# Weight conversion spread over a step, an early rescale on ScalarE, and single eighths in two of nine steps

## The chip, the cores and the metric

The kernel runs on one core of a Trainium2 chip. Time is that of one execution on the device, in microseconds; a kernel's time is the median of its runs. A profiled execution is traced by the hardware profiler, and its span runs from the first to the last instruction of the program.

## The reference

Three layers follow one another on float32 data: attention that keeps the 32 highest scores of each row, a gated feed-forward layer, and a layer of eight experts in which each token goes to one. Cut to what matters:

```python
# attention: 4 batches, 8 heads, 576 rows, 64 wide
scores = q @ k.T / sqrt(64)
kth = np.partition(scores, -32, axis=-1)[..., -32:-31]
scores = np.where(scores >= kth, scores, -1e9)
attn = exp(scores - scores.max(-1))
attn = attn / (attn.sum(-1) + 1e-9)
x = attn @ v                          # as 2304 tokens of 512
# feed-forward: w_in 512x2048, w_out 2048x512, given as float64
h = x @ w_in
x = (h * clip(h + 3, 0, 6) / 6) @ w_out
# experts: each token to the one of 8 with the highest logit, 512 -> 1024 -> 512
out[mask] = gate[mask] * (relu(x[mask] @ w1[e]) @ w2[e])
```

## The kernel before

**Steps and units.** Attention is cut into 72 units: 64 of two heads by 128 query rows (`t`), and 8 for the remaining rows of four heads (`r`). A loop of 76 steps runs them as a pipeline of five stages written out by hand: step i makes the scores of unit i (stage 0), selects the 32 highest of unit i-1 on VectorE, masks unit i-2, exponentiates and rescales unit i-3, and transposes unit i-4 and multiplies it with V. The order in which `step` calls the pieces is the order of each engine's instructions; every engine takes its own in order and waits at semaphores for the others. Four score buffers `s` go round.

Per step, VectorE runs four rounds of MAX and MATCH_REPLACE (`select`, L354 and L357), the reciprocal of the row sums (L388) and `pairs` (L335 to L339), which halves the rows that the next `select` looks at. `pairs` reads the score copy that ScalarE makes (`take`, L326) and the scores in PSUM, and TensorE can write the next scores only when it is through. ScalarE also does `relu` (L371), `expo` (L381) and the copies of the transposes (`keep`, L410); GpSimd does `mask` (L375) and the rescale (`scale`, L394).

**Feed-forward work in the same steps.** A group of 128 tokens is finished with each fourth `t` unit of a batch and row block (two more groups with the last `r` unit), and puts eight eighths into the queue `moe`; an eighth is 256 of the 2048 hidden columns. A step takes up to two, `a` and `b`: `s1` is 16 products with w_in into PSUM (L463), `gate`, `swish`, `large` and `small` (L468 to L479) make the gated value in two parts, and `s2` is six products with w_out (L488). Of `a`, all of it stands in one step; the `s2` of `b` stands in the next step, as `last`. A step that finds the queue empty starts none. What is left after the loop is taken by a loop behind it, ahead of the experts.

**Weight conversion.** w_in and w_out arrive as 64-bit words, in 64 pieces of 128x256, each by a DMA into one of five raw buffers (`load_w`). `convert_w` takes two pieces: VectorE shifts and masks the high words (L194, a TENSOR_SCALAR) and joins the sign (L196); then, for three of four pieces, ScalarE scales the low word (L199) and GpSimd adds it (L200), for the fourth VectorE joins it (L202). A w_in piece is finished with that. A w_out piece goes into a buffer `wf` of a ring of four that it shares with the gate's tile `u`; ScalarE then rounds it into `wh` (L204) and GpSimd puts the rest into `wl` (L205), in the same call. The calls stand at the end of a step: two in steps 0 to 3, three in steps 4 to 7, four from step 8, so the 64 pieces are through with step 10.

Of the kernel before, what the change touches and what calls it, by code (L numbers as in the profile page):

```python
# [25 lines left out]
CH = 256  # L26
# [8 lines left out]
BIG = 2.0 ** 100  # L35
NUNIT = 72
NS = 4
HS = S // 2
QS = S // 4
SCALE = 1.0 / 8.0  # L40
# [23 lines left out]
def layers(ctx: ExitStack, tc: tile.TileContext, qt, kt, v, w_in, w_out, embt, tau, w1, w2, out, y_dram, g_dram, x_dram, tbl, flag):  # L64
# [93 lines left out]
    for q in range(8):  # L158
        for k in range(4):
            c = slice(256 * q, 256 * q + 256)  # L160
            wpieces.append((w_in[128 * k:128 * k + 128, c], win[:, k, c], None))
        for k in (2 * q, 2 * q + 1):
            for c in (slice(0, 256), slice(256, 512)):
                wpieces.append((w_out[128 * k:128 * k + 128, c], wh[:, k, c], wl[:, k, c]))
    wraw = deque()
    cnt = [0]

    def load_w():
# [11 lines left out]
    def convert_w():  # L180


        plain, words = [], []
        for raw, dst, rest, single in [wraw.popleft() for _ in range(min(2, len(wraw)))]:
            full = dst if rest is None else mp.tile([128, 256], F32, tag="ug", name="wf", bufs=4)
            if single:
                nc.vector.tensor_copy(full, raw)
            else:
                cnt[0] += 1
                words.append((raw, full.bitcast(I32), cnt[0] % 4 != 3))  # L190
            if rest is not None:
                plain.append((full, dst, rest))
        for raw, t, _ in words:
            nc.vector.tensor_scalar(t, raw[:, :, 1], 3, 0x3FFFFFF8, op0=ALU.logical_shift_left, op1=ALU.bitwise_and)  # L194
        for raw, t, _ in words:
            nc.vector.scalar_tensor_tensor(t, raw[:, :, 1], -0x40000000, t, op0=ALU.bitwise_and, op1=ALU.bitwise_or)  # L196
        for raw, t, rounded in words:
            if rounded:
                nc.scalar.activation(raw[:, :, 0], raw[:, :, 0].bitcast(U32), AF.Copy, scale=2.0 ** -29)  # L199
                nc.gpsimd.tensor_tensor(t, t, raw[:, :, 0], op=ALU.add)  # L200
            else:
                nc.vector.scalar_tensor_tensor(t, raw[:, :, 0], 29, t, op0=ALU.logical_shift_right, op1=ALU.bitwise_or)  # L202
        for full, hi, lo in plain:
            nc.scalar.copy(hi, full)  # L204
            nc.gpsimd.tensor_tensor(lo, full, hi.bitcast(F32), op=ALU.subtract)  # L205
        load_w()

# [91 lines left out]
    def lows():  # L301
        while low:
            o, x, h = low.popleft()
            nc.gpsimd.tensor_tensor(o, x, h, op=ALU.subtract)
        while low2:
            o, x, h = low2.popleft()
            nc.vector.tensor_tensor(o, x, h, op=ALU.subtract)  # L307
# [82 lines left out]
    def scale(i):  # L390
        rv = sums.pop(i)
        for n in range(2):
            x = tile_of(i, n)
            nc.gpsimd.tensor_scalar(x, x, rv[:, n:n + 1], 1.0, op0=ALU.mult, op1=ALU.mult)  # L394

    tb_ = {}

# [56 lines left out]
    def push_group(X, g):  # L454
# [9 lines left out]
            state[q, "h"] = ph.rearrange("p a n -> p (a n)")  # L464

        def gate(q):
            state[q, "u"] = u = mp.tile([128, CH], F32, tag="ug", name="u", bufs=4)
            nc.scalar.activation(u, state[q, "h"], AF.Relu, bias=half, scale=1.0 / 6.0)  # L468

        def swish(q):  # L470
# [223 lines left out]
    def step(i, last):  # L694
        def at_(j, f, *a):
            if 0 <= i - j < NU:
                f(i - j, *a)

        a = moe.popleft() if moe else None
        b = moe.popleft() if moe else None  # L700
        part(last, 4)
        part(last, 5)
        at_(2, relu, 0)
        at_(2, mask, 0)
        at_(3, expo, 0)
        lows()
        load_k(i + 2)
        at_(1, select, 0)
        at_(1, select, 1)
        part(a, 1)  # L710
        part(a, 2)
        part(a, 3)
        for c in range(2):
            at_(4, turned, c)
            at_(4, keep, c)
        at_(0, scores, 0)
        at_(4, turned, 2)
        at_(4, keep, 2)
        at_(0, take, 0)
        at_(1, select, 2)  # L720
        at_(3, expo, 1)
        at_(3, guard)
        part(last, 6)
        part(a, 4)
        part(a, 5)
        at_(0, scores, 1)
        at_(0, take, 1)
        at_(1, select, 3)
        at_(3, inverse)
        at_(3, scale)  # L730
        at_(2, relu, 1)
        at_(2, mask, 1)
        at_(1, bounds)
        part(b, 1)
        at_(0, pairs)
        part(b, 2)
        part(b, 3)
        load_q(i + 3)
        if i + 1 < NU and units[i + 1][0] == "r":
            prep(i + 1)  # L740
            lows()
        if i + 2 < NU and units[i + 2][0] != "r":
            prep(i + 2)
        at_(4, values)
        part(a, 6)
        at_(4, finish)
        need_v(i)
        if side:
            side.popleft()()
        if i == 1:  # L750
            setup()
        if i == 5:
            embed()
        for _ in range(2 if i < 4 else 3 if i < 8 else 4):
            convert_w()
        return b or a

    if True:
        for t in zq:
# [232 lines left out]
```

## Time and profile before

| | |
|---|---|
| median of 3 runs | 1216.61 us (1215.84 to 1221.48) |
| the profiled execution | 1215.63 us, its span 1213.9 us |
| TensorE (PE) products busy | 1045.8 us, 86% of the span |
| VectorE (DVE) busy | 835.2 us, 69% |
| ScalarE (ACT) busy | 735.2 us, 61% |
| GpSimd (POOL) busy | 664.9 us, 55% |

Busy time is a mean over stages: the first 200 us convert weights, the next 600 run attention and feed-forward together, and the last 400 the rest of the feed-forward layer and the experts. Products are pipelined and their ends modelled, so a busy TensorE is not one at its peak. An idle gap is put down to the engine or DMA whose signal came last before it ended.

### The profile page before, as it was taken

To read this page: it belongs to the slowest core of one execution; us is meant where nothing else is said; L and a number is where in the kernel's file an instruction comes from. 1 tells how busy PE (TensorE), PEld (TensorE's weight loads), DVE (VectorE), ACT (ScalarE), POOL (GpSimd) and SP (SyncE) were. 2 spreads that over 40 slices of the span, in tenths; PEclk is the share of its full clock that TensorE was granted. 3 is DMA by queue.
4 is the path that set the end of the run, shared out by engine and by line. 5 is a ranking of instruction groups with operands and counts; after the bars stand their busy time and mean duration, and the time that the engine had idled before them with its cause. 6 is when DMAs were issued, how large, how long until landed. Compare 5 with 4: busy or idle time off the path is not lost.

```text
span 1213.9 us, 22599 instructions
## 1 busy us (share of the span) xinstructions
PE 1045.8 (86%) x7800; PEld 927.7 (76%) x7800; DVE 835.2 (69%) x2718; ACT 735.2 (61%) x1628; POOL 664.9 (55%) x950
## 2 busy tenths in 40 slices
PE   2244659998999989999998999999998899999993
PEld 1133548887989878899887999988987788877882
DVE  6989777899878799887989878861234343444540
ACT  4455547787777788777777777774344343443540
POOL 5767666687666687766778567663330343221200
PEclk9976778999999999999999999999998999999997
DMA  7433230131000132000131000100040564333530
GB/s 221 136 94 122 89 100 25 47 82 55 11 27 25 32 91 62 10 28 25 42 86 56 10 27 21 30 10 10 10 165 10 173 213 177 133 132 123 186 140 21
DMA packets 71782, 92.75 MB, mean 76 GB/s; under 512 B 18319, under 2 KB 44066, under 8 KB 71647
## 3 DMA queue, kind: packets, MB, share of 16 engines
q1 hardware_dynamic: 67007, 81.00, 21.1%
q0 software_dynamic: 4640, 10.10, 2.5%
q8 instruction: 66, 1.08, 0.4%
q14 instruction: 69, 0.57, 0.2%
HBM read 80.37 MB, written 11.32 MB: 76 GB/s over the span
## 4 chain that ended last, share of the span: by engine, by line
PE 46%; issue 10%; DMA 8%; DVE 7%; ACT 5%; POOL 2%; SPq 1%; POOLq 0%; ACTq 0%; DVEq 0%
PE bank_h L463 15%; PE y L488 13%; PE bank_a L423 5%; DMA out_dram<-ob,idt 5%; PE ps_sc L323 4%; PE bank_t L405 3%; PE ph L821 3%; DVE A L354 2%; PE po L834 2%; DMA a<-in_moe_w_dram 1%; PE bank_t L517 1%; DVE left L357 1%; ACT s L381 1%; DMA xg<-y_dram,idt 1%; DVE kst L307 1%
## 5 line engine op out<-in xcount | busy, mean ns | idle before, releaser
L463 PE MATMUL bank_h<-x,win 128*128 128x128 f32 x2304 | 291.4, 279 | 5.0 <-ACT x L443 3.6
L463 PEld LDWEIGHTS bank_h<-x,win 128*128 128x128 f32 x2304 | 280.7, 195 | 12.0 <-ACT x L443 4.3
L375 POOL TENSOR_TENSOR s<-s,z 128x576 f32<-128x576 f32 x144 | 185.5, 1288 | 3.7 <-ACT z L371 3.5
L405 PE MATMUL bank_t<-ident,s 128*128 128x128 f32 x648 | 102.2, 286 | 79.4 <-ACT pt L410 71.4
L354 DVE MAX8 A<-left 128x8 f32<-128x288 f32 (+1 forms) x288 | 160.2, 598 | 0.0
L479 POOL TENSOR_TENSOR gl<-u,gh 128x256 fp32r<-128x256 f32 x144 | 106.5, 740 | 84.2 <-ACT gh L476 78.3
L405 PEld LDWEIGHTS bank_t<-ident,s 128*128 128x128 f32 x648 | 76.2, 147 | 89.1 <-ACT pt L410 79.1
L468 ACT ACTIVATE u<-bank_h,half 128x256 f32<-128x256 f32 x144 | 68.0, 472 | 110.0 <-PE bank_h L463 106.2
L488 PE MATMUL y<-wh,gh 128*128 128x512 f32 x288 | 128.9, 447 | 0.0
L323 PE MATMUL ps_sc<-kst,qh 128*128 128x288 f32 x256 | 85.0, 345 | 43.5 <-ACT s L326 24.1
L394 POOL TENSOR_SCALAR s<-s,sums 128x576 f32<-128x576 f32 x144 | 106.4, 749 | 24.0 <-DVE sums L388 23.9
L488 PE MATMUL y<-wh,gl 128*128 128x512 f32 x288 | 116.2, 403 | 0.0
L472 DVE SCALAR_TENSOR_TENSOR u<-u,bank_h 128x256 f32<-128x256 f32 x144 | 59.9, 416 | 81.4 <-ACT u L468 80.5
L488 PE MATMUL y<-wl,gh 128*128 128x512 f32 x288 | 115.2, 400 | 0.0
L653 DVE TENSOR_TENSOR l<-a,h 128x1024 fp32r<-128x1024 f32 x64 | 76.7, 1222 | 56.0 <-ACT h L652 55.8
L371 ACT ACTIVATE z<-s,zb 128x576 bf16<-128x576 f32 x144 | 112.5, 781 | 0.0
L410 ACT COPY pt<-bank_t 128x384 f32<-128x384 f32 x216 | 96.2, 480 | 26.7 <-PE bank_t L405 26.7
L381 ACT ACTIVATE s<-s,nb 128x576 f32<-128x576 f32 x144 | 111.8, 776 | 0.0
L326 ACT COPY s<-ps_sc 128x576 f32<-128x576 f32 x144 | 92.9, 645 | 17.0 <-PE ps_sc L323 17.0
L423 PE MATMUL bank_a<-pt,vt 128*64 128x128 f32 (+1 forms) x1600 | 99.5, 274 | 0.0
L385 POOL TENSOR_SCALAR sums<-sums 128x2 f32<-128x2 f32 x72 | 15.9, 220 | 148.9 <-ACT s L381 148.0
L323 PEld LDWEIGHTS ps_sc<-kst,qh 128*128 128x128 f32 x256 | 52.5, 205 | 57.1 <-ACT s L326 19.7
(222 smaller groups left out, 2513.4 us busy)
## 6 DMA issues: line engine op xcount, KB each, us to landing
a<-in_moe_w_dram SPq DMA_DIRECT2D x64, 512.0 KB, 7.9
kraw<-in_k_dram SPq DMA_DIRECT2D x64, 144.0 KB, 2.5
qraw<-in_q_dram SPq DMA_DIRECT2D x64, 128.0 KB, 2.2
w<-in_moe_w_in_dram SPq DMA_DIRECT2D x32, 256.0 KB, 3.1
w<-in_moe_w_out_dram SPq DMA_DIRECT2D x32, 256.0 KB, 2.8
vt<-in_v_dram SPq DMA_DIRECT2D x16, 320.0 KB, 3.1
y_dram<-ysb SPq DMA_DIRECT2D x18, 256.0 KB, 2.0
qraw<-in_q_dram SPq DMA_DIRECT2D x16, 64.0 KB, 2.0
```

Of the source, the lines that this page charges most:

```text
L323: nc.tensor.matmul(ps[:, n, :HS], t, kk[:, HS * g:HS * g + HS], start=(o == 0), stop=(o == len(parts) - 1))
L354: nc.vector.max(A[:, n, 8 * r:8 * r + 8], src[:, n, :w])
L371: nc.scalar.activation(zb_[n], tile_of(i, n), AF.Relu, bias=sel[i][2][:, n:n + 1], scale=-BIG)
L375: nc.gpsimd.tensor_tensor(s, s, zb_[n], op=ALU.subtract)
L381: nc.scalar.activation(s, s, AF.Exp, bias=sel[i][1][:, n:n + 1], scale=SCALE, accum_out=sums[i][:, n:n + 1])
L394: nc.gpsimd.tensor_scalar(x, x, rv[:, n:n + 1], 1.0, op0=ALU.mult, op1=ALU.mult)
L405: nc.tensor.transpose(pp[:, 128 * k:128 * k + 128], e[:, 128 * (3 * c + k):128 * (3 * c + k) + 128], ident)
L410: nc.scalar.copy(pts[i][:, 3 * c:3 * c + 3, :].rearrange("p k n -> p (k n)"), tb_.pop((i, c))[:, :384])
L423: nc.tensor.matmul(av[64 * n:64 * n + 64, c0:c1], vt[:, k, 64 * n:64 * n + 64], pt[:, k + 5 * n if k < 4 else 4, c0:c1], start=(o == 0), s ...
L463: nc.tensor.matmul(ph[:, a, :], win[:, k, 128 * f:128 * f + 128], X[:, k, :], start=(k == 0), stop=(k == 3))
L479: nc.gpsimd.tensor_tensor(state[q][1], state.pop((q, "u")).rearrange("p (a n) -> p a n", a=2), state[q][0].bitcast(F32), op=ALU.subtract)
L488: nc.tensor.matmul(state["y"], x[:, a, :], w[:, f, :], start=(f == 0 and n == 0), stop=(f == 15 and n == 2))
```

## The change

`convert_w` makes the words only: a w_out pair goes into one 512-wide buffer `both` of the pool of the token tiles (`xp`, four buffers) and into a list; a new `split_w`, called once a step after `lows`, rounds and subtracts what stands in the list, 512 columns at a time. The calls of `convert_w` are no longer one after another at the end: a step has four places (`words`), and takes the first two, three or four of them, as many calls as before. For units 0 to 8, `scale` runs on ScalarE and stands later in the step. In steps with i % 9 of 2 or 6, `b` is not taken. The gate's ring has three buffers.

```diff
+EARLY = 9
...
-                wpieces.append((w_out[128 * k:128 * k + 128, c], wh[:, k, c], wl[:, k, c]))
+                wpieces.append((w_out[128 * k:128 * k + 128, c], None, (wh[:, k, :], wl[:, k, :])))
     wraw = deque()
+    whole_w = deque()
...
-        plain, words = [], []
-        for raw, dst, rest, single in [wraw.popleft() for _ in range(min(2, len(wraw)))]:
-            full = dst if rest is None else mp.tile([128, 256], F32, tag="ug", name="wf", bufs=4)
+        words, two = [], [wraw.popleft() for _ in range(min(2, len(wraw)))]
+        if two and two[0][2] is not None:
+            both = xp.tile([128, DM], F32, tag="x", name="wf")
+        for o, (raw, dst, rest, single) in enumerate(two):
+            full = dst if rest is None else both[:, 256 * o:256 * o + 256]
...
-        for full, hi, lo in plain:
+        if two and two[0][2] is not None:
+            whole_w.append((both,) + two[0][2])
+        load_w()
+
+    def split_w():
+
+        while whole_w:
+            full, hi, lo = whole_w.popleft()
             nc.scalar.copy(hi, full)
             nc.gpsimd.tensor_tensor(lo, full, hi.bitcast(F32), op=ALU.subtract)
-        load_w()
...
-            nc.gpsimd.tensor_scalar(x, x, rv[:, n:n + 1], 1.0, op0=ALU.mult, op1=ALU.mult)
+            if i < EARLY:
+                nc.scalar.activation(x, x, AF.Copy, scale=rv[:, n:n + 1])
+            else:
+                nc.gpsimd.tensor_scalar(x, x, rv[:, n:n + 1], 1.0, op0=ALU.mult, op1=ALU.mult)
...
-            state[q, "u"] = u = mp.tile([128, CH], F32, tag="ug", name="u", bufs=4)
+            state[q, "u"] = u = mp.tile([128, CH], F32, tag="ug", name="u", bufs=3)
...
+        more = iter(range(2 if i < 4 else 3 if i < 8 else 4))
+
+        def words():
+            if next(more, None) is not None:
+                convert_w()
+
+
         a = moe.popleft() if moe else None
-        b = moe.popleft() if moe else None
+        b = moe.popleft() if moe and i % 9 not in (2, 6) else None
...
         lows()
+        split_w()
         load_k(i + 2)
         at_(1, select, 0)
         at_(1, select, 1)
         part(a, 1)
         part(a, 2)
         part(a, 3)
+        words()
...
         at_(1, select, 2)
+        words()
...
         at_(3, inverse)
-        at_(3, scale)
+        if i - 3 >= EARLY:
+            at_(3, scale)
...
         part(b, 1)
         at_(0, pairs)
+        words()
         part(b, 2)
...
+        if i - 3 < EARLY:
+            at_(3, scale)
         at_(4, values)
...
-        for _ in range(2 if i < 4 else 3 if i < 8 else 4):
-            convert_w()
-        return b or a
+        words()
+        return b
```

On VectorE, around the end of step 8 of the kernel before, the conversion stands in one piece behind the last row of `pairs` and the `swish` of the second eighth (`w` are the raw buffers, `win` the finished w_in, `wf` the w_out words):

```order
L339 TENSOR_TENSOR left<-ps_sc,left 128x2x144
L472 SCALAR_TENSOR_TENSOR u<-u,bank_h_118 128x256
L194 TENSOR_SCALAR win<-w_1039 128x256
L194 TENSOR_SCALAR win<-w_1055 128x256
L196 SCALAR_TENSOR_TENSOR win<-w_1039,win 128x256
L196 SCALAR_TENSOR_TENSOR win<-w_1055,win 128x256
L194 TENSOR_SCALAR win<-w_1057 128x256
L194 TENSOR_SCALAR win<-w_1072 128x256
L196 SCALAR_TENSOR_TENSOR win<-w_1057,win 128x256
L196 SCALAR_TENSOR_TENSOR win<-w_1072,win 128x256
L202 SCALAR_TENSOR_TENSOR win<-w_1057,win 128x256
L194 TENSOR_SCALAR wf<-w_1074 128x256
```

In step 9 of the changed kernel, a call stands between the third and the fourth round of `select`, and the reciprocal and `pairs` come behind it (line numbers are those of the changed file):

```order
L198 SCALAR_TENSOR_TENSOR win<-w_1170,win 128x256
L362 MAX A<-left 128x8 x2
L365 MATCH_REPLACE left<-A,left 128x288 x2
L196 TENSOR_SCALAR win<-w_1172 128x256
L196 TENSOR_SCALAR win<-w_1211 128x256
L198 SCALAR_TENSOR_TENSOR win<-w_1172,win 128x256
L198 SCALAR_TENSOR_TENSOR win<-w_1211,win 128x256
L204 SCALAR_TENSOR_TENSOR win<-w_1172,win 128x256
L362 MAX A<-left 128x8 x2
L368 TENSOR_SCALAR zb<-A 128x1 x2
L396 RECIPROCAL sums<-sums 128x2
L343 TENSOR_TENSOR ps_sc<-ps_sc,s_144 128x2x144
```

What moved: two calls of a step of eight pieces now stand ahead of `pairs`, a third right behind it and ahead of `swish`, and the fourth at the end.

On ScalarE, at the turn from step 9 to step 10 of the kernel before, scaling of low words and casts of `wh` stand in a row, ahead of the next step's `large` (L476), `relu` (L371) and `expo` (L381):

```order
L443 COPY x<-bank_a 128x128
L199 ACTIVATE w_1218<-w_1218 128x256
L199 ACTIVATE w_1234<-w_1234 128x256
L199 ACTIVATE w_1251<-w_1251 128x256
L199 ACTIVATE w_1253<-w_1253 128x256
L199 ACTIVATE w_1384<-w_1384 128x256
L204 CAST wh<-wf 128x256 x2
L199 ACTIVATE w_1395<-w_1395 128x256
L204 CAST wh<-wf 128x256 x2
L476 CAST gh<-u 128x256
L371 ACTIVATE z_151<-s_143,zb 128x576
L381 ACTIVATE s_146,sums<-s_146,nb 128x576
```

In the changed kernel, at the end of step 9 and the start of step 10, the rescale (L403) stands behind the cast of the queries, one scaling of a low word follows, and the casts of `wh` come behind the next step's `relu` and `expo`:

```order
L479 ACTIVATE u<-bank_h_118,half 128x256
L303 CAST qh<-qraw 128x256
L403 ACTIVATE s_145<-s_145,sums 128x576 x2
L454 COPY x<-bank_a 128x128
L201 ACTIVATE w_1292<-w_1292 128x256
L487 CAST gh<-u 128x256
L379 ACTIVATE z_151<-s_143,zb 128x576
L389 ACTIVATE s_146,sums<-s_146,nb 128x576
L213 CAST wh<-wf 128x512 x2
L479 ACTIVATE u<-bank_h_117,half 128x256
L201 ACTIVATE w_1294<-w_1294 128x256
L201 ACTIVATE w_1345<-w_1345 128x256
```

What moved: nothing of a w_out piece waits any more for words of the same call, and two rescales of 576 columns are new in the row.

On TensorE, at the end of step 33 of the kernel before, the second eighth's `s1` (L463) stands between the scores and V's products; step 34, which starts no eighth, then has the `s2` of that one alone:

```order
L323 MATMUL ps_sc<-kst,ql 128x288
L463 MATMUL bank_h_118<-x,win 128x128 x8
L423 MATMUL bank_a<-pt,vt 64x128 x10
L488 MATMUL y<-wh,gh 128x512
L488 MATMUL y<-wl,gh 128x512
```

In the changed kernel, step 33 (33 % 9 is 6) has no second `s1`, and step 34 does not lack its first:

```order
L331 MATMUL ps_sc<-kst,ql 128x288
L434 MATMUL bank_a<-pt,vt 64x128 x10
L499 MATMUL y<-wh,gh 128x512
L499 MATMUL y<-wl,gh 128x512
L499 MATMUL y<-wh,gl 128x512
L499 MATMUL y<-wh,gh 128x512
L499 MATMUL y<-wl,gh 128x512
L499 MATMUL y<-wh,gl 128x512
L528 MATMUL bank_t_120<-ent,yt 128x8 x4
L474 MATMUL bank_h_118<-x,win 128x128 x8
```

What moved: one `s1` is missing from step 33, and one `s2` (the `last` of that eighth) from step 34, where before two `s1` and one `s2` were missing from step 34 and one `s2` from step 35.

## Rows read from the trace of the kernel before

**Rows 1.** The page: busy time of the engines, and VectorE's busy tenths in 40 slices.
```profile
PE 1045.8 (86%) x7800; PEld 927.7 (76%) x7800; DVE 835.2 (69%) x2718; ACT 735.2 (61%) x1628; POOL 664.9 (55%) x950
...
DVE  6989777899878799887989878861234343444540
```

**Rows 2.** Windows of the conversion stage: start and end, length, then as headed.
```profile
core 0: us, PE busy (x) PEld busy (x) DVE busy (x) ACT busy (x) POOL busy (x), PEclk, DMA share, GB/s
17.50:59.90 42.40, 10.18 (x33) 7.52 (x33) 42.16 (x135) 19.27 (x45) 32.27 (x50) 1.00 0.52 163
59.90:124.00 64.10, 28.66 (x176) 23.42 (x176) 55.94 (x172) 37.68 (x87) 43.81 (x62) 0.68 0.35 107
124.00:185.70 61.70, 36.31 (x243) 32.69 (x244) 46.89 (x145) 33.05 (x82) 41.87 (x60) 0.75 0.28 88
```

**Rows 3.** Waits from 59.9 to 197.5: us in total, times, longest.
```profile
PE bank_t L405 <- ACT pt L410: 54.6, 7, 8.2
...
ACT wh L204 <- POOL wf L200: 13.4, 18, 4.3
...
DVE ps_sc L335 <- ACT s L326: 9.3, 7, 1.9
...
DVE u L472 <- ACT u L468: 6.8, 5, 1.9
```

**Rows 4.** Timeline of one conversion block: start, us, engine, line; in brackets idle before.
```profile
134.94 0.43 ACT L199 ACTIVATE w<-w 128x256 int32<-128x256 uint32 x1 [2.76 <-DMA w<-in_moe_w_out_dram]
...
137.92 0.80 DVE L194 TENSOR_SCALAR wf<-w 128x256 int32<-128x256 int32 x1 [1.30 <-POOL wl L205]
...
139.76 0.41 ACT L204 CAST wh<-wf 128x256 fp32r<-128x256 f32 x1 [1.62 <-DVE wf L202]
...
143.32 0.90 PE L405 MATMUL bank_t<-ident,s 128*128 128x128 f32 x3 [8.23 <-ACT pt L410]
```

**Rows 5.** Windows after the conversion, columns as in Rows 2.
```profile
197.50:798.80 601.30, 580.54 (x4901) 521.52 (x4900) 518.51 (x1900) 460.42 (x1078) 422.26 (x625) 0.99 0.14 40
...
391.80:402.20 10.40, 10.40 (x87) 9.51 (x86) 8.02 (x32) 7.55 (x18) 7.76 (x11) 1.00 0.05 13
402.20:412.90 10.70, 10.48 (x87) 9.30 (x86) 8.13 (x31) 8.37 (x21) 6.71 (x10) 1.00 0.06 14
412.90:421.90 9.00, 9.00 (x75) 8.01 (x74) 6.91 (x27) 7.02 (x17) 6.66 (x10) 1.00 0.30 83
421.90:430.20 8.30, 6.54 (x58) 5.54 (x56) 8.10 (x24) 7.99 (x21) 5.15 (x8) 1.00 0.25 74
430.20:441.90 11.70, 9.58 (x100) 8.57 (x101) 11.60 (x47) 8.47 (x22) 9.13 (x14) 1.00 0.33 88
```

**Rows 6.** L194: groups from 17.5 to 197.5; then minimum, median, maximum ns.
```profile
L194 DVE TENSOR_SCALAR wf<-w 128x256 int32<-128x256 int32 x32 | 16.4, 533 | 6.3 <-POOL wl L205 3.9 <-DMA w<-in_moe_w_out_dram 2.4
L194 DVE TENSOR_SCALAR win<-w 128x256 int32<-128x256 int32 x28 | 16.0, 614 | 0.0
...
L194 DVE TENSOR_SCALAR win<-w x32: 279/814/844, 14.1 to 173.4; 128x256 int32<-128x256 int32 x32
```

**Rows 7.** The page's costliest groups: busy us, mean ns, idle before.
```profile
L394 POOL TENSOR_SCALAR s<-s,sums 128x576 f32<-128x576 f32 x144 | 106.4, 749 | 24.0 <-DVE sums L388 23.9
L371 ACT ACTIVATE z<-s,zb 128x576 bf16<-128x576 f32 x144 | 112.5, 781 | 0.0
```

**Rows 8.** Timeline of the start, columns as in Rows 4.
```profile
11.88 0.47 DVE L335 TENSOR_TENSOR ps_sc<-ps_sc,s 128x288 f32<-128x288 f32 x1 [2.28 <-ACT s L326]
...
14.15 0.48 DVE L194 TENSOR_SCALAR win<-w 128x256 int32<-128x256 int32 x2
...
16.29 0.42 DVE L202 SCALAR_TENSOR_TENSOR win<-w,win 128x256 int32<-128x256 int32 x1
```

**Rows 9.** Chain behind the loop of steps, in order of time: start, us, what.
```profile
848.54 1.78 PE bank_h L463 x16
...
866.85 1.38 PE y L488 x6
```

More of the change, by code (lines that the diff above doesn't have):

```diff
@@ L190, in convert_w @@
                 words.append((raw, full.bitcast(I32), cnt[0] % 4 != 3))
-            if rest is not None:
-                plain.append((full, dst, rest))
         for raw, t, _ in words:
```

## The prediction

> **What bounds the kernel now.** I read the page first: TensorE is busy 86% of the span and VectorE 69%, but the row of VectorE's slices shows 9 and 8 in the first slices, and 3 to 5 after two thirds of the span [rows 1]. So there are stages. The windows of the first 200 us, cut where ScalarE's first score copy of steps 1, 4, 8 and 11 starts, show which engine fills each [rows 2]. From 17.5 to 59.9 VectorE is busy 42.16 of 42.40 us: nothing but less work on VectorE helps there. From 59.9 to 124.0 it is busy 55.94 of 64.1 (8.2 idle), from 124.0 to 185.7 (three steps of eight weight pieces, 20.6 us each) 46.89 of 61.7 (14.8 idle). No other engine is near full in these: ScalarE 33.05, GpSimd 41.87, TensorE 36.31 of 61.7, and that at a mean granted clock of 0.75, between the two levels of 1.2 and 2.4 GHz (0.5 and 1.0). Later steps of two eighths take 10.4 and 10.7 [rows 5], 10.5 in the mean. So the stage waits on a chain across engines.
>
> The waits of this stage name the links [rows 3]: TensorE's last transposes wait 54.6 us for ScalarE's copy of the first (7 times, about 8 us each), ScalarE's cast of a w_out piece waits 13.4 for GpSimd's add, VectorE's `pairs` (L335) waits 9.3 for ScalarE's score copy, and `swish` (L472) waits 6.8 for the gate. One conversion block shows why [rows 4]: ScalarE waits 2.76 us for a weight load, VectorE 1.30 for a `wf` buffer that GpSimd frees, ScalarE again 1.62 for VectorE; its next step's work is queued behind, so TensorE has sat idle 8.23 us when its transposes start at 143.32. The block is serial, and the four engines stand in it by turns.
>
> After 197.5 TensorE is the bound: busy 580.54 of 601.3 us, 20.8 idle, at clock 0.99 [rows 5]. In a step of 10.7 TensorE is busy 10.48; the step without any (34) and its successor take 9.0 and 8.3, and the steps with new keys after it 11.7 with VectorE at 11.60. The idle time of TensorE lies around the steps with no eighth and with new keys.
>
> **The change, part by part.** *Conversion spread over the step.* Every piece keeps its VectorE work; what can go is VectorE's 23.0 idle us (8.2 + 14.8). By cause [rows 3, 6]: 6.3 before L194 (3.9 for a buffer, 2.4 for a load), 9.3 at `pairs`, 6.8 at `swish`; 22.4 of it.
> - The 6.3 go: the 512-wide buffers are freed by `split_w` early in the next step, and a load has a quarter of a step more until its call comes.
> - At `pairs`, two calls now stand between the start of `select` and `pairs`. Their four L194 alone are 4 x 0.57 = 2.3 us (the mean of 533 and 614 ns, [rows 6]), more than the longest wait of 1.9 [rows 3], and ScalarE does not come out of a block late. I let 8 of 9.3 go and keep 1.3 for the steps where ScalarE is late by itself.
> - `swish` of the second eighth has a call ahead of it now, that of the first still stands where it stood: half of 6.8 goes, 3.4.
> - At the start, the two calls of step 0 come before its `pairs`. VectorE takes 14.15 to 16.71 for these words, 2.6 us, but sits idle 2.28 before `pairs` there already [rows 8]. The cost is 0 to 2.6; I take 0.7, near the lower end, since loads still have to land.
>
> Sum of the stage: 6.3 + 8 + 3.4 - 0.7 = 17.0 us gained. Bounds: only the 6.3 go and the start costs all (3.7 gained); or all 23.0 go, and with them what L194 loses now over its shortest: 32.4 - 60 x 0.279 = 15.7 [rows 6], together 38.7. I take 17, the value by causes.
>
> *Rescale on ScalarE for units 0 to 8.* It takes 18 x 0.749 = 13.5 us from GpSimd and puts 18 x 0.78 = 14.1 on ScalarE, by the row of an ACTIVATE of the same 128x576 [rows 7]. In the three long steps that is 3 x 1.56 = 4.7: ScalarE 37.8 busy of some 50 us, so covered, with 12 to spare; uncovered it would cost 14.1. It stands behind the next query cast, and the transposes that read it are a step later. Twice 512 instead of four times 256 columns in the split is off the path on both engines: no gain counted, no loss. The gate's tile has three buffers instead of four, with two taken in a step: nothing.
>
> *The shared port.* On w_in pieces L194 takes 279 ns at the least, 814 at the median and 844 at the most [rows 6]: half of them are held for half a microsecond. The Trainium skill, "SBUF — State Buffer", section "SBUF: two separate sides", says that VectorE in a two-port mode and GpSimd take one port pair in turn and the later one blocks for the whole instruction. The trace agrees so far (279 against 814 ns), and the rule speaks against the change: the calls now meet GpSimd's masks and splits as well. By the present means the stage gains 17; by the rule at its worst, with every L194 blocked, it gains nothing, which is the first rival below.
>
> *Eighths.* From step 12 on the kernel before starts 116 eighths in 64 steps, with six steps of none; the changed one 113, with fifteen steps of one and none of zero (counted with the queue's rule: 8 per finished group of tokens). Steps 8 to 11 start 7 instead of 8, the loop behind starts 24 instead of 20. An eighth costs TensorE 1.78 + 1.38 = 3.16 us [rows 9]: 4 x 3.16 = 12.6 are added behind, and the same 12.6 are taken from steps, where TensorE is the bound. These cancel, and what is left is TensorE's idle time of 20.8. In a step without eighths TensorE lacks 2 x 1.78 + 1.38 at once, which is under what the other engines need (9.0 and 8.3). With one eighth it lacks 1.78 in that step and 1.38 in the next: 10.5 - 1.78 = 8.7 and 9.1, about at the 8.3 to 9.0 that the others need. So most of the idle time at empty steps goes. What stays is that of steps with new keys, where VectorE is full: 1.76 + 2.12 us in two windows [rows 5], over three batches 11.6. I take 10 gained of 20.8. Bounds: all 20.8 gained; or 7 lost, if a step of one eighth saves half of what an empty step and its successor do against 10.5 (1.5 + 2.2 = 3.7): 15 x 1.85 = 27.8 saved, where before 6 x 3.7 = 22.2 were, and 12.6 more behind the loop.
>
> **Sum.** The profiled execution took 1215.63 us; 1215.6 - 17 - 10 = 1188.6. The median of the runs, 1216.61, is 1.0 above the profiled one, so 1189.6, rounded 1190.
>
> **The rivals.** (1) *The port eats it.* Every L194 at 0.814: 64 x 0.814 = 52 against 33.4 now (32.4 for 60 of them [rows 6], and about 0.25 for each of the first four [rows 8]), 18 us more on a VectorE that is now the bound; the 17 are gone and with 10 to 0 from the eighths it ends at 1207 to 1218. For it: the median of 0.814 now. Against: GpSimd has 13.5 us less to do. (2) *The waits move with the work.* ScalarE and GpSimd take all in order, so a cast or a rescale that waits for VectorE may hold the score copy as the block did; only the 6.3 and half of the idle time at empty steps go: 1215.6 - 6 - 5 + 1 = 1206. For it: ScalarE waits 13.4 for GpSimd now. Against: casts are a step behind their adds. (3) *Nothing but work is left*: the upper bounds of both parts by three quarters, 1216 - 29 - 15 = 1172. For it: no engine but VectorE is full. (4) *Slower: steps of one eighth are as long as steps of two.* If another engine's chain holds them at 10.5, fifteen steps save nothing, the empty steps' savings are lost (22.2 us), and the added 12.6 stay: +35 against -17 from the stage, 1234 at worst, 1224 if they save 0.7 us each. It decides from about 1.2 us saved per step of one eighth: 15 x 1.2 = 18 = 35 - 17. Against it: VectorE is busy 8.13 of 10.7 in a step of two, and steps did fall to 8.3 [rows 5]. That the conversion is not spread at all is excluded by the order of the rows.
>
> **Numbers.** Forecast as above 0.62 (its own range 1180 to 1202), rival 1 0.08, rival 2 0.10, rival 3 0.15, rival 4 0.05. The range from 1174 to 1207 leaves out the outer half of rival 3, most of rival 1, and rival 4, 2 in 10. A measurement of this kernel tells 0.5% (6 us) from no change: faster is below 1210.5. Rival 1 is mostly within, half of rival 2's spread too: faster 0.85, same 0.10, slower 0.05.
>
> **What would show it.** The step of eight pieces at 16.5 to 17.5 us instead of 20.6, with VectorE over 0.92 busy; no wait of the shift instructions for GpSimd and hardly one for loads; TensorE's wait for the transposes' copy under 3 us instead of 8; the new rescale at 0.78 us on ScalarE; the steps of one eighth at 8.7 to 9.3 with TensorE over 0.95 busy; four more eighths at 3.2 behind the loop. Wrong would make it: a mean of the shift instructions over 0.7 us, ScalarE waiting in front of its score copies for GpSimd or VectorE, or steps of one eighth over 10 us.

## The result and the profile after

| | before | after |
|---|---|---|
| median of the runs on one chip | 1216.22 us (4 runs) | 1197.0 us (4 runs, 1196.62 to 1197.87) |
| span of the profiled execution | 1213.9 us | 1196.1 us |
| start of step 12 (ScalarE's first score copy) | 197.5 | 176.4 |
| start of step 71 | 798.8 | 770.4 |
| TensorE idle between these two | 20.8 | 23.1 |

The ratio to the kernel before is 0.9833 (95% interval 0.9806 to 0.9861), some 19 to 20 us faster. 1190 was forecast. The forecast had 17 us from the conversion stage and 10 from the loop behind it. The traces give 21.1 us by the start of step 12, and a net loss of 3.3 after it: the loop from step 12 to 71 became 7.3 shorter (601.3 to 594.0), the part behind it 10.6 longer (415.1 to 425.7), of which 0.8 is the experts' part (293.5 to 294.3, from the last product with w_out to the end).

The page after, to be held against [rows 1]: busy time of the engines, and VectorE's busy tenths.

```profile
PE 1047.7 (88%) x7800; PEld 927.0 (78%) x7800; DVE 829.1 (69%) x2718; ACT 741.1 (62%) x1630; POOL 651.0 (54%) x916
...
DVE  6979997998888898888898888922225343444440
```

The means hardly moved. The windows show the stages, cut at the same steps as [rows 2, 5] (steps 1, 4, 8, 11, 12 and 71):

```profile
core 0: us, PE busy (x) PEld busy (x) DVE busy (x) ACT busy (x) POOL busy (x), PEclk, DMA share, GB/s
18.70:56.80 38.10, 10.23 (x33) 7.53 (x33) 37.88 (x134) 19.64 (x42) 24.36 (x37) 1.00 0.51 166
56.80:116.90 60.10, 31.75 (x176) 26.10 (x176) 53.13 (x168) 41.06 (x89) 36.62 (x49) 0.66 0.37 115
116.90:165.90 49.00, 35.89 (x243) 30.95 (x244) 48.90 (x146) 34.82 (x80) 36.85 (x49) 0.84 0.35 111
...
176.40:770.40 594.00, 570.90 (x4852) 512.70 (x4853) 514.89 (x1898) 456.16 (x1074) 420.75 (x623) 1.00 0.15 40
```

Three steps of eight pieces take 49.0 us instead of 61.7, and VectorE is busy 48.90 of them: the stage that waited on a chain across engines is now full on one engine. From step 1 to 11, 168.2 us became 147.2: VectorE's idle time fell from 23.2 us to 7.3 (147.2 less 139.9 busy), its busy time from 145.0 to 139.9, and 7.0 of the idle time that is left lies in the middle window. The waits from 18.7 to 176.4 name the links that went, beside [rows 3]:

```profile
PE bank_t L416 <- ACT pt L421: 19.9, 7, 4.2
...
ACT w L201 <- DMA w<-in_moe_w_out_dram: 7.3, 6, 4.0
...
ACT wh L213 <- POOL wf L202: 3.1, 4, 1.5
...
DVE ps_sc L343 <- ACT s L334: 1.0, 1, 1.0
DVE u L483 <- ACT u L479: 1.0, 1, 1.0
```

The transposes' wait for ScalarE's copy fell from 54.6 to 19.9, the cast's for GpSimd from 13.4 to 3.1, `pairs` from 9.3 to 1.0, `swish` from 6.8 to 1.0.

One step stands out: step 5 took 22.2 us, where it took 16.7 before (step 6 then took 9.7 instead of 14.6). It runs `embed`, which loads the experts' embedding, squares and normalizes it. The timeline there (start, us, engine, line; idle before in brackets; SPq is SyncE's DMA queue, whose time includes its wait):

```profile
74.25 5.17 SPq L179 DMA_DIRECT2D w<-in_moe_w_out_dram  x3
...
81.04 0.47 SPq L123 DMA_DIRECT2D et<-in_moe_expert_emb_dram  x1
83.52 0.19 DVE L127 TENSOR_TENSOR sq<-et 128x32 f32<-128x32 f32 x1 [4.31 <-DMA et<-in_moe_expert_emb_dram]
...
83.86 1.84 PE L130 MATMUL bank_a<-sq,onesf 128*128 128x8 f32 x8 [10.00 <-DVE sq L127]
85.74 0.18 ACT L132 ACTIVATE nr<-bank_a 128x8 f32<-128x8 f32 x1 [7.39 <-PE bank_a L130]
85.95 0.23 DVE L133 TENSOR_SCALAR nr<-nr,tb 128x8 f32<-128x8 f32 x1 [2.24 <-ACT nr L132]
```

The embedding's load stands on SyncE's queue behind weight loads that wait for a raw buffer, so it goes out at 81.04; VectorE then waits 4.31 us for it, TensorE 10.00 for VectorE, ScalarE 7.39 for TensorE, and VectorE 2.24 for ScalarE. The two waits of VectorE, 6.55 us, are nearly all of the 7.0 idle in that window.

Last, the shift and join of the words, and GpSimd's subtraction, by groups from 18 to 176 us (us busy, mean ns), beside the shift's groups in [rows 6]:

```profile
L214 POOL TENSOR_TENSOR wl<-wf,wh 128x512 fp32r<-128x512 f32 x16 | 22.6, 1430 | 0.8 <-DVE wf L198 0.7
L198 DVE SCALAR_TENSOR_TENSOR win<-w,win 128x256 int32<-128x256 int32 x28 | 19.7, 743 | 0.0
...
L196 DVE TENSOR_SCALAR win<-w 128x256 int32<-128x256 int32 x28 | 13.8, 532 | 0.0
...
L198 DVE SCALAR_TENSOR_TENSOR wf<-w,wf 128x256 int32<-128x256 int32 x32 | 13.1, 447 | 0.0
...
L196 DVE TENSOR_SCALAR wf<-w 128x256 int32<-128x256 int32 x32 | 11.9, 412 | 0.0
```

The shift got shorter (it was 533 and 614 ns in [rows 6]), but the join of the w_in pieces has a mean of 743, with 408 as its shortest. The four groups together are 58.5 us.

### The profile page after: what moved, and what is told of

It is laid out like the page before. It is cut to its first block, busy times and chain, and to the rows that moved or that the text cites. A ratio compares the mean times of both kernels' runs of the same rounds, so it can differ in the third digit from the quotient of the medians.

```text
span 1196.1 us, 22551 instructions
## 1 busy us (share of the span) xinstructions
PE 1047.7 (88%) x7800; PEld 927.0 (78%) x7800; DVE 829.1 (69%) x2718; ACT 741.1 (62%) x1630; POOL 651.0 (54%) x916
## 4 chain that ended last, share of the span: by engine, by line
PE 56%; DVE 15%; issue 10%; DMA 9%; ACT 5%; POOL 2%; SPq 0%; POOLq 0%; DVEq 0%; ACTq 0%
PE bank_h L474 17%; PE y L499 16%; PE bank_a L434 6%; PE ps_sc L331 5%; PE bank_t L416 4%; DMA out_dram<-ob,idt 4%; DVE A L362 3%; PE po L858 3%; DMA xg<-y_dram,idt 2%; PE ph L845 2%; DVE left L365 2%; DVE win L198 2%; DMA a<-in_moe_w_dram 1%; ACT pt L421 1%; PE bank_t L528 1%
## 5 line engine op out<-in xcount | busy, mean ns | idle before, releaser
L474 PE MATMUL bank_h<-x,win 128*128 128x128 f32 x2304 | 289.0, 277 | 4.2 <-ACT x L454 4.2
L474 PEld LDWEIGHTS bank_h<-x,win 128*128 128x128 f32 x2304 | 278.9, 193 | 10.9 <-ACT x L454 4.5
L379 ACT ACTIVATE z<-s,zb 128x576 bf16<-128x576 f32 x144 | 112.7, 783 | 10.8 <-DVE zb L368 10.8
L334 ACT COPY s<-ps_sc 128x576 f32<-128x576 f32 x144 | 92.9, 645 | 13.5 <-PE ps_sc L331 13.5
L405 POOL TENSOR_SCALAR s<-s,sums 128x576 f32<-128x576 f32 x126 | 93.3, 751 | 10.6 <-DVE sums L396 10.5
L663 ACT CAST h<-a 128x1024 fp32r<-128x1024 f32 x64 | 65.4, 1048 | 46.3 <-DMA a<-in_moe_w_dram 23.5
```

Source lines behind the costliest of these rows:

```text
L379: nc.scalar.activation(zb_[n], tile_of(i, n), AF.Relu, bias=sel[i][2][:, n:n + 1], scale=-BIG)
L474: nc.tensor.matmul(ph[:, a, :], win[:, k, 128 * f:128 * f + 128], X[:, k, :], start=(k == 0), stop=(k == 3))
```

## The experiments

The theory after the result: the stage gained by the two-phase conversion as forecast, and lost some of it in step 5; single eighths saved only the work that they took out, because TensorE waits elsewhere in such steps. Rivals: single eighths gained and the stage lost it; or the port that VectorE and GpSimd share holds the stage. In the runs below the kernel before took 1219.6 to 1220.4 us, so ratios to it are what is compared.

**Two eighths in every step, in the changed kernel.**

```diff
-        b = moe.popleft() if moe and i % 9 not in (2, 6) else None
+        b = moe.popleft() if moe else None
```

> The changed kernel, but b is always taken, so steps of two eighths as before. Prediction's theory (single eighths fill TensorE's idle time, 10 us gained): 1207 us, 10 slower than the changed kernel. New theory (a step behind a single eighth has no s2 left over from b to put between the two halves of its scores, so TensorE waits 1.1 us there, and in all the single eighths cost about 3 us): 1193 to 1195 us.

Measured 1199.39 us, ratio 0.9829 (0.9807 to 0.985): the same as with single eighths, so neither theory's time came. **Single eighths alone, in the kernel before:**

```diff
-        b = moe.popleft() if moe else None
+        b = moe.popleft() if moe and i % 9 not in (2, 6) else None
...
-        return b or a
+        return b
```

> The kernel before with nothing but the single eighths in steps with i % 9 of 2 or 6. Prediction's theory: 1206 us, 10 faster than before. New theory: 1217 to 1220, 1 to 4 slower than before, with 15 waits of 1.1 us between the halves of the scores where there were 6.

Measured 1219.09 us, ratio 0.9986 (0.9969 to 1.0003), no change that the runs can tell; in its profile the loop takes 592.3 us instead of 601.3, and the rest 427.7 instead of 415.1 (4.6 of it in the experts' part, which the edit does not touch). The 15 waits of 1.1 us are there. So by both sides single eighths are worth nothing, to within the some 5 us that such an interval is wide, and the gain belongs to the conversion and the rescale.

Why, the waits of the changed kernel from 176.4 to 770.4 say:

```profile
PE ps_sc L331 <- ACT s L334: 16.6, 15, 1.1
...
PE bank_t L416 <- ACT pt L421: 4.9, 14, 1.5
```

TensorE waits 15 times 1.1 us for ScalarE's score copy; in the kernel before, from 197.5 to 798.8, it was six times:

```profile
PE ps_sc L323 <- ACT s L326: 6.7, 6, 1.1
```

Where these waits stand, the timeline of the changed kernel shows (here at 358 to 361):

```profile
358.56 0.49 PE L416 MATMUL bank_t<-ident,s 128*128 128x128 f32 x3
360.15 0.40 PE L331 MATMUL ps_sc<-kst,qh 128*128 128x288 f32 x1 [1.11 <-ACT s L334]
...
360.80 1.95 PE L474 MATMUL bank_h<-x,win 128*128 128x128 f32 x16
```

The second half of the scores (`scores` 1) may be written only when `take` has copied the first. Between the two, TensorE's row has the last transposes and, in most steps, the left-over `s2` of the step before (`last`). In the step behind a single eighth there is no left-over, so the copy is uncovered, and the `s1` of `b` (L474) stands only behind it.

**The gap filled.** In steps with no left-over, the `s1` of `b` goes between the halves of the scores:

```diff
         part(last, 6)
+        if last is None:
+            part(b, 1)
...
-        part(b, 1)
+        if last is not None:
+            part(b, 1)
```

> The changed kernel with one move: in a step that has no s2 left over from the step before, the s1 of b stands between the two halves of the scores instead of behind the bounds. If the uncovered wait of 1.1 us (15 times) is what takes the single eighths' gain: 8 to 14 us gained, about 0.974 of the kernel before. Rival (those steps are held by VectorE or ScalarE anyway, TensorE's wait is only where the slack shows): under 3 us gained, 0.981 to 0.984.

Measured 1185.51 us, ratio 0.972 (0.9701 to 0.9739), 11 to 14 us better than the changed kernel (by the medians and by the ratios). Its waits from step 12 to 71 hold one of this kind:

```profile
PE ps_sc L331 <- ACT s L334: 1.1, 1, 1.1
```

The window of the same stretch, columns as above:

```profile
175.25:753.47 578.22, 566.58 (x4849) 509.63 (x4848) 514.83 (x1898) 454.21 (x1074) 421.21 (x623) 1.00 0.15 41
```

And TensorE's timeline at the same place in the program:

```profile
351.27 0.49 PE L416 MATMUL bank_t<-ident,s 128*128 128x128 f32 x3
351.59 1.95 PE L474 MATMUL bank_h<-x,win 128*128 128x128 f32 x16
353.30 0.38 PE L331 MATMUL ps_sc<-kst,qh 128*128 128x288 f32 x1
```

The waits of 16.6 us are down to 1.1, and TensorE's idle time in the loop to 11.6 (578.22 less 566.58). **The gap filled with two eighths in every step**, which parts the filling from the single eighths:

> The changed kernel with a second eighth in every step as before, and in steps with no left-over eighth the second eighth's first product between the two halves of the scores. It tells whether the filling alone gains or only together with single eighths. Theory (single eighths earn what was forecast as soon as the wait for the score copy is covered): only the steps behind an empty step gain, 6 or 7 times about 1 us, so about 1192 us, and single eighths with the filling (1185.5) are worth some 7 more. Rival (filling is the whole gain and single eighths add nothing): about 1185.

Measured 1193.88 us, ratio 0.978 (0.9757 to 0.9804). By these the filling alone gains 5 to 6 us on the kernel with two eighths, and single eighths on top of it gain 7 to 8. The profiles, from the start of step 12 to the last product with w_out, part it otherwise: 722.3 us with two eighths, 719.4 with the filling, 708.1 with single eighths and the filling, which is 2.9 and 11.3. Either way single eighths need the filling; the filling gains less without them.

**The embedding's loads early**, at the end of step 2 instead of in `embed`:

```diff
+        if i == 2:
+            embed_loads()
...
         if i == 5:
             embed()
```

> The changed kernel with the two small loads of embed issued at the end of step 2 instead of step 5. Theory that the 22.2 us of step 5 are these loads waiting on SP's queue behind a weight load that has no buffer yet: step 5 falls to about 15, 6 to 7 us gained, 1190 to 1191. Rival (VectorE only shifts its work, the stage being full): under 1 us gained, 1196 to 1197.

Measured 1195.84 us, ratio 0.9808 (0.9788 to 0.9829). Step 5 takes 18.2 us instead of 22.2, and step 12 starts at 170.8 instead of 176.4. The whole time shows 0.5 to 3 us of this, with intervals that overlap those of the changed kernel: nearer to the rival's time than to the 1190 to 1191 of the theory, though the stage gained 5.6 us, nearly what the theory said. In this profile the experts' part takes 299.0 us instead of 294.3. The wait for the load is gone, a chain through three engines is left:

```profile
79.51 1.85 PE L127 MATMUL bank_a<-sq,onesf 128*128 128x8 f32 x8 [5.99 <-DVE sq L124]
81.40 0.18 ACT L129 ACTIVATE nr<-bank_a 128x8 f32<-128x8 f32 x1 [3.40 <-PE bank_a L127]
81.61 0.23 DVE L130 TENSOR_SCALAR nr<-nr,tb 128x8 f32<-128x8 f32 x1 [2.24 <-ACT nr L129]
```

**Both edits together** (their diffs above):

> The changed kernel with both edits that gained by themselves: in a step with no left-over eighth the first product of the second eighth stands between the two halves of the scores, and the embedding's two small loads are issued at the end of step 2. Theory (two separate waits, one in the steps after single eighths, one in step 5): the gains add up, 14 and 3 us, about 1182 us. Rival (both took the same idle time of TensorE, since a later start of the queue of eighths only moves work behind the loop): no more than the first edit alone, about 1185.5.

Measured 1182.12 us, ratio 0.9677 (0.965 to 0.9704): by the medians the gains add up (3.4 us below the filling alone, with intervals that just meet; step 12 starts at 172.4 instead of 175.3), and this is the fastest kernel here that computes the whole result. **The changed kernel again**, unaltered, beside it:

> The changed kernel unaltered, as the measure for the experiments on this chip: 1196 to 1199 us by every theory, which is what its earlier runs gave (1197.0).

Measured 1196.35 us, ratio 0.982 (0.9789 to 0.9851).

**The conversion's parts.** First all calls of `convert_w` at the end of the step again, `split_w` still a phase of its own:

```diff
         part(a, 3)
-        words()
...
         at_(1, select, 2)
-        words()
...
         at_(0, pairs)
-        words()
...
-        words()
+        for _ in range(4):
+            words()
```

> The changed kernel with the word calls all at the end of the step again, the split still a phase of its own in the next step. Theory that spreading is what frees VectorE: the steps of eight pieces go back to about 20 us and steps 4 to 7 to 15 to 17, 1210 to 1214 us, 0.994 of the kernel before. Rival (the two phases alone break the chain of ScalarE and GpSimd): 1200 us, 0.985, with steps of eight pieces at 17.

Measured 1208.91 us, ratio 0.992 (0.9901 to 0.9939). The steps of eight pieces take 19.8 us, as expected, and step 12 starts at 188.0. The transposes wait 43.7 us, where [rows 3] has 54.6, by the waits from 18 to 176 us:

```profile
PE bank_t L416 <- ACT pt L421: 43.7, 7, 7.7
```

Then spread over the step, but with the split in the same call:

```diff
             whole_w.append((both,) + two[0][2])
+            split_w()
```

> The changed kernel with the split in the same call as the words, at the four places. Theory that the second phase matters because ScalarE otherwise waits for GpSimd's add in front of its next work: steps of eight pieces at 18 to 19 us, 6 to 8 us slower, 0.989 of the kernel before. Rival (spreading alone is enough, since VectorE does not wait for ScalarE or GpSimd): 0.983, no change.

Measured 1213.09 us, ratio 0.9946 (0.9927 to 0.9965): 14 to 17 us slower than the changed kernel, twice what was expected. The steps of eight pieces take 17.7 us, steps 4 to 7 70.1 instead of 60.1. ScalarE's cast now waits 47.0 us for GpSimd, 3.1 in the changed kernel, by the waits from 18 to 182 us:

```profile
ACT wh L214 <- POOL wf L202: 47.0, 16, 5.8
```

Against the kernel before, the second phase without the spreading gives 11 us, the spreading without the second phase 7, both together 20 to 23 (each with the other edits of the change in it). What each half gains alone is not idle time: from step 1 to 11 VectorE is idle 26.8 us with the calls at the end (159.7 less 132.9 busy) and 36.0 with the split in the same call (158.4 less 122.4), more than the 23.2 of the kernel before, while shift and join take 49.0 and 44.6 us instead of 60.2. Only both together bring the idle time down, to 7.3, and there shift and join stay at 58.5. Spreading puts more engines' waits into the middle of the step, and it pays only when ScalarE does not wait there for a chain that VectorE and GpSimd have just begun.

**The rescale on GpSimd again:**

```diff
-EARLY = 9
+EARLY = 0
```

> The changed kernel with the rescale of all units on GpSimd, at its old place. Prediction's term (off the path on both engines): 1197, no change. Rival (GpSimd's 18 instructions hold the port against VectorE, which is full in steps 8 to 10, and stand ahead of the adds): 3 to 6 us slower, 1200 to 1203, with L196 and L198 longer in the mean.

Measured 1202.2 us, ratio 0.9858 (0.9838 to 0.9879), 3 to 6 us slower than the changed kernel, as the rival had it, and step 12 starts at 180.6 instead of 176.4. Shift and join take 63.0 us together (14.2 + 14.5 + 21.3 + 13.0) instead of 58.5, and the transposes' wait for the copy stays (19.0). VectorE is busy 144.2 us from step 1 to 11 instead of 139.9, and idle 7.5 instead of 7.3. So those 4 us are VectorE time beside a busier GpSimd.

**The port.** In the changed kernel, the joins of 1.5 us stand beside GpSimd's subtraction. VectorE's timeline first, then GpSimd's:

```profile
131.36 1.21 DVE L196 TENSOR_SCALAR win<-w 128x256 int32<-128x256 int32 x2
132.49 2.92 DVE L198 SCALAR_TENSOR_TENSOR win<-w,win 128x256 int32<-128x256 int32 x2
135.34 0.81 DVE L362 MAX8 A<-left 128x8 f32<-128x288 f32 x2
```

```profile
131.65 0.77 POOL L312 TENSOR_TENSOR ql<-qraw,qh 128x256 fp32r<-128x256 f32 x1
132.38 2.75 POOL L214 TENSOR_TENSOR wl<-wf,wh 128x512 fp32r<-128x512 f32 x2
135.09 1.61 POOL L202 TENSOR_TENSOR win<-win,w 128x256 int32<-128x256 int32 x2
```

Two joins run from 132.49 to 135.41, two subtractions from 132.38 to 135.13: each join takes about as long as the subtraction beside it. It is not the subtraction as such. Here a join starts 0.11 us behind an add (L202) of the changed kernel and takes 0.95 us, again VectorE first, then GpSimd:

```profile
58.97 0.95 DVE L198 SCALAR_TENSOR_TENSOR win<-w,win 128x256 int32<-128x256 int32 x1
```

```profile
58.86 0.78 POOL L202 TENSOR_TENSOR win<-win,w 128x256 int32<-128x256 int32 x1
```

What counts is who starts first. Of the twelve joins in this trace that start while a subtraction or an add runs on GpSimd, ten end 0.28 us after it (the other two stand beside a subtraction that itself took 2.25 us). Ten more joins meet only an add that starts after them, and take 0.41 to 0.42 us. First, **the subtraction in two halves** of 256 columns:

```diff
-            nc.gpsimd.tensor_tensor(lo, full, hi.bitcast(F32), op=ALU.subtract)
+            for c in (slice(0, 256), slice(256, 512)):
+                nc.gpsimd.tensor_tensor(lo[:, c], full[:, c], hi[:, c].bitcast(F32), op=ALU.subtract)
```

> The changed kernel with GpSimd's split subtraction in two halves of 256 columns instead of one of 512. Theory that VectorE's L198 (mean 743 ns on w_in pieces, at most 1510) is held for the rest of GpSimd's 1.43 us instruction: the mean falls to about 600 and the longest to under 1000, 2 to 4 us gained, 0.981. Rival (the same GpSimd time in two pieces holds as much): 0.983 to 0.985, GpSimd's work is no shorter.

Measured 1200.46 us, ratio 0.9848 (0.9826 to 0.987), no gain. The joins of the w_in pieces did what the theory said (607 ns in the mean, 956 the longest), but those of the w_out pieces grew (482 ns instead of 447, the longest 1493). Shift and join still take 56.4 us (58.5 in the changed kernel), and the halves of the subtraction cost more in sum, 26.9 against 22.6 us. Its groups from 18 to 186 us:

```profile
L215 POOL TENSOR_TENSOR wl<-wf,wh 128x256 fp32r<-128x256 f32 x32 | 26.9, 867 | 0.8 <-DVE wf L198 0.7
...
L198 DVE SCALAR_TENSOR_TENSOR win<-w,win 128x256 int32<-128x256 int32 x28 | 15.9, 607 | 0.0
```

Then **the subtraction taken off GpSimd**:

```diff
-            nc.gpsimd.tensor_tensor(lo, full, hi.bitcast(F32), op=ALU.subtract)
+            nc.scalar.activation(lo, full, AF.Copy, scale=0.0)
```

> The changed kernel with GpSimd's 512-wide subtraction of a w_out pair left out: ScalarE writes zeros into that low part instead, so the low part of w_out is missing from the result (16 instructions move from GpSimd to ScalarE). Theory (the subtraction of 1.33 to 1.43 us holds VectorE's join beside it, which takes 1.5 us instead of 0.41): the join's longest falls below 0.9 us, its mean from 0.6 towards 0.42, and since VectorE is the bound in the conversion stage, step 12 begins 5 to 8 us earlier and the time is about 1190 us. Rival (the hold belongs to whatever GpSimd runs there, since its next instruction moves up beside the joins): the longest stays above 0.9, shift and join together lose less than 3 us, and the time stays at 1194 to 1200; ScalarE's added 16 x 0.7 us could even make it slower.

Measured 1184.34 us, ratio 0.9704 (0.9685 to 0.9722), 12 us below the changed kernel by the medians (14 to 16 by the ratios), twice what was expected. The join of the w_in pieces, by minimum, median and maximum in ns:

```profile
L198 DVE SCALAR_TENSOR_TENSOR win<-w,win x32: 409/412/422, 11.8 to 142.7; 128x256 int32<-128x256 int32 x32
```

And the groups from 18.7 to 165.9 us:

```profile
L198 DVE SCALAR_TENSOR_TENSOR wf<-w,wf 128x256 int32<-128x256 int32 x32 | 12.0, 417 | 0.0
L196 DVE TENSOR_SCALAR wf<-w 128x256 int32<-128x256 int32 x32 | 11.9, 414 | 0.0
L198 DVE SCALAR_TENSOR_TENSOR win<-w,win 128x256 int32<-128x256 int32 x28 | 10.5, 413 | 0.0
L214 ACT ACTIVATE wl<-wf 128x512 fp32r<-128x512 f32 x16 | 10.0, 626 | 0.0
L196 DVE TENSOR_SCALAR win<-w 128x256 int32<-128x256 int32 x28 | 9.8, 390 | 0.0
```

No join is held any more: in this trace none starts while a GpSimd instruction runs. The four groups sum to 44.2 us instead of 58.5, 14.3 less, and step 12 starts at 162.5 instead of 176.4, 13.9 earlier: with VectorE full, what an instruction is held comes one to one out of the time. Behind step 12 the two profiles take nearly the same (1021.4 us here, 1019.7 in the changed kernel), so the zeros in the low part gain nothing there. The shift still takes longer at times (its mean of 414 and 390 stands over a shortest of 279 and 276).

## Why the prediction came near, and which step of it failed

*The conversion stage: mechanism right, the term undersized.* 17 us were forecast, 21.1 came by step 12. The sum priced VectorE's idle time alone; of the 21.0 us from step 1 to 11, 15.9 are idle time and 5.1 a VectorE that is less busy, which the sum did not have. Its causes went as listed: the waits of `pairs` fell by 8.3 (8 forecast), of `swish` by 5.8 (3.4), and the shift waits no more for GpSimd. The steps of eight pieces came to 16.3 us in the mean, with VectorE full (16.5 to 17.5 forecast). The transposes' wait came to 2.8 us in the mean, 4.2 at the longest, where under 3 was named. Both halves of the mechanism were needed, as the idle times of the two experiments on the parts show. Two terms were missing. The embedding's load cost the stage some 5 us (with early loads step 12 starts 5.6 earlier; the longer step 5 alone does not show it, since step 6 is shorter): the prediction went through the queues of compute engines, and did not ask what else stands behind the weight loads on SyncE's queue. Against it stands the rescale.

*Rescale: "covered", counted 0; worth 3 to 6.* The sum asked whether ScalarE has room for 14.1 us, and it had. It did not price what GpSimd's 13.5 us do to VectorE, although it read the 814 ns of [rows 6] as VectorE held by GpSimd; it named the 13.5 us only as an argument against rival 1. The run with the rescale back on GpSimd has 4.5 us more in shift and join, most of the 5.1 above.

*The port: rival 1 half right.* The shifts were not held more than before, but what the prediction priced was the shift alone. The joins took the hold over: their longest was 1.51 us (0.95 before), and the four groups of shift and join take 58.5 us where the same four took 60.2 before. In the kernel before, VectorE had idle time beside it; that the hold cost less there was not tested. Now it is time: 12 to 14 us, as the run without the subtraction shows. The upper bound of the stage, 38.7, did count the hold of the shifts. The Trainium skill, "SBUF — State Buffer", section "SBUF: two separate sides", names in the same rule, besides the two-port modes, a VectorE operation with two SBUF inputs, against a GpSimd operation that reads SBUF: whichever starts first has the port pair for its whole instruction, and the other blocks. The joins agree (0.41 us when they start first, 1.5 us behind a subtraction of 1.3 to 1.5). The prediction used only the part on two-port modes.

*Eighths: the step that failed.* "With one eighth it lacks 1.78 in that step and 1.38 in the next: 10.5 - 1.78 = 8.7 and 9.1, about at the 8.3 to 9.0 that the others need. So most of the idle time at empty steps goes." These are the windows of such a step (24) and the next, columns as above, first in the kernel before, then in the changed one:

```profile
319.20:329.10 9.90, 9.90 (x83) 9.01 (x82) 9.56 (x36) 7.19 (x18) 5.97 (x9) 1.00 0.01 2
329.10:339.60 10.50, 10.50 (x89) 9.43 (x88) 8.88 (x35) 7.71 (x20) 7.50 (x12) 1.00 0.06 15
```

```profile
300.40:308.50 8.10, 7.66 (x64) 6.60 (x62) 7.88 (x33) 6.17 (x16) 5.28 (x8) 1.00 0.00 0
308.50:319.00 10.50, 9.83 (x84) 9.00 (x85) 9.43 (x38) 7.80 (x20) 7.53 (x12) 1.00 0.06 16
```

The first half came true: 8.1 us where the same step took 9.9 before. The second did not: the next, from 308.50 on, takes 10.5 as before, where 9.1 was counted on, with TensorE 0.67 idle (with the 0.44 idle at the end of the window before, this is the wait of 1.1). The two steps together lack 3.16 of products and save 1.8. The 1.38 of `s2` that the second lacks was the cover of ScalarE's score copy. Fifteen steps with a wait of 1.1 took the place of six. TensorE's idle time in the loop rose from 20.8 to 23.1, where 10.8 was forecast. The loop's 7.3 us are fewer products (TensorE 9.6 less busy), paid back behind the loop. This is rival 4 in a mild form, and its price was zero, not a loss: inside the bounds that the term was given, from 7 lost to 20.8 gained, but not the 10 that was picked. With the gap filled the forecast came nearly true: idle 11.6, and 7 to 8 us gained of 10.

So by the profiled spans the stage gave 4.1 us more than forecast and the rest 13.3 less (-3.3 where +10 stood), 9.2 in all; by the medians the forecast was 7 us too low. The terms missing in the stage, about -5 for the embedding and +3 to 6 for the rescale, nearly cancelled, and the stage's surplus made up part of what the eighths did not give. That 1197 lies so near to 1190 is in part luck.

## What to carry to other kernels

- A product that is taken out of a step may have been the cover of somebody else's latency. Before counting it as saved, read which wait stands next to it in the engine's row; then put other work there. Here the same single eighths gave 0 without and 7 to 8 us with such a filling.
- When an edit fills an engine, what was harmless beside it becomes time: price what holds its instructions (mean against shortest), for every kind of instruction it has, and what a step's other DMAs stand behind.
- Deferring the second half of a chain by a step and spreading the first half over the step gave 11 and 7 us alone and 20 to 23 together, and only together took idle time from VectorE; neither is judged by itself.

## What the runs showed of the hardware

- A VectorE instruction with two inputs (SCALAR_TENSOR_TENSOR, 128x256 int32) takes 0.41 us alone, or when it starts before its GpSimd neighbour. Started 0.1 to 0.3 us behind one that reads two tiles, it ended 0.28 us after it in ten of twelve cases: 1.48 to 1.51 us beside a 128x512 subtraction, 0.95 beside a 128x256 add. Without the subtractions the longest of 64 was 0.422; with the subtraction cut in two it took 0.94 to 0.95 beside a half.
- The experts' part at the end (from the last product with w_out) is the same in all these kernels, yet it took 292.0 to 300.4 us from profile to profile, at a mean granted clock of 0.93 to 0.96. A single profile's end is uncertain by some 4 us either way for that reason; differences between these kernels are better read at the start of step 12 and of step 71, or from medians.
